# Operands of the first MoE's projection read straight into their low tiles, rounded on ScalarE, with the side weights and staged loads set wider apart in the attention

## The chip, the cores and the metric

The kernel runs on one core of one Trainium2 chip. The metric is the device time of one execution in microseconds (us). Of the kernel before there are three timed runs: 907.71, 910.16 and 914.64 us, median 910.16 us.

## The reference

Three layers in a row, all in float32: an attention with a decay bias, a mixture with a maximum of three products, and a mixture with a product of two.

```
scores = q @ k.T / sqrt(64);  bias = min(-(cum_i - cum_j), 0), cum = cumsum(max(s, 0))
attn = softmax(where(causal, scores + bias, -1e9)) @ v        # 4 batches, 8 heads, 576 x 64
x  = attn laid out as 2304 tokens x 512
h1 = max(x @ w1, x @ w2, x @ w3)                              # 2304 x 768
x2 = h1 @ w_out                                               # 2304 x 512, "the projection"
hT = (x2 @ w_a) * (x2 @ w_b)                                  # 2304 x 1536
out = hT @ w2_out                                             # 2304 x 512
```

## The kernel before

Every product of the MoE layers is made of three matmuls on TensorE: an operand `a` is split into `hi = round(a)` and `lo = a - hi` (the helper `hilo`: the rounding by `rnd` on ScalarE, letter A, or GpSimd, letter P; the subtraction always on VectorE), and `hi*hi + hi*lo + lo*hi` are added up in PSUM.

**Attention with the first MoE's gates (about 0 to 433 us).** Eight steps, one for a batch and one of its two ranges of rows (256 or 320 columns). A list called `stream` holds pairs of a position and a function: position 2.4 is 40% through step 2. It is sorted by position, and its functions are emitted in that order. The gates of a step (`gate`, 18 of them, 12 matmuls each, PSUM tile `g`, three banks) run one step later, as the other work of TensorE beside the attention of the next step; for each block of h1 ScalarE copies the first gate out of PSUM (L768), VectorE takes the maximum with the other two (L771), and ScalarE's queue sends the block to DRAM as `h1T` (L774). A scheduler then orders the instructions on each engine by priority and its own model of the time; each engine works its queue in that order. SyncE (SP) issues nearly all loads, in one queue.

Two kinds of side work stand in `stream` too. The **side weights** (w_out, six pieces, and two pieces of w_a and w_b) are loaded by `fetch_w1` into the ring `wst` of three buffers and turned to float32 by `load_side` (one instruction on ScalarE, two on VectorE); `w20_side` and `wsums` make sums and splits of them. The **staged sums**: the projection uses a scheme with seven products where eight would be needed (`OPS`, products 1, 2, 6, 5, 7, 4, 3), so four of its seven operands are sums of quarters of h1. For the first two of three blocks of 768 tokens, `stage_load` reads four quarters back from `h1T` into the one buffer `st`, `stage_sum` makes the four sums on VectorE and stores them as `h1S`; six such pieces (k = 0 to 5). Heads of the attention are loaded by `load_pair` (L510: `kraw`, the transposed keys), two pairs ahead, and split by `split_qk`, whose first instruction of the keys is a rounding on ScalarE into `KB`.

**The tail of the gates (400 to 433 us).** The last 18 gates run alone on TensorE. Beside them the seven operands of the projection's first block are read into the two buffers `hr` (`h_fetch`), rounded on ScalarE and GpSimd in turn (`HE`), and subtracted (`h0_make`); the weights of the projection are rounded on GpSimd (`wo1_make`).

**The projection (433 to 504 us).** `run_sb(sb)` makes a block of 768 tokens: seven products for each of two halves, 9 matmuls each (`chain`, L1115). The products 1, 6, 7, 4 add up in PSUM tile X, 2 in Y, 5 and 3 in Z, with one bank of each for either half, and a copy to `xt` by ScalarE (L1156, L1160, L1162, L1187) or an addition by VectorE between. Operands of the second block come through the four buffers `hrB` (`h1_fetch`), each rounded and subtracted into a slot A to F when the space for it is free (`freed`, `h_make`); those of the third through the same buffers, with four sums on VectorE (`h_sums`). `x0_split` splits the first block's result for the next layer.

**The second MoE (504 to 912 us)** follows the same pattern, and the change doesn't touch it.

Of the kernel before, what the change touches and what calls it, by code (L numbers as in the profile page):

```python
# [8 lines left out]
F32 = mybir.dt.float32  # L9
# [20 lines left out]
def kernel(  # L30
# [29 lines left out]
    P = 128  # L60
# [14 lines left out]
    def f(ap):  # L75
        return ap.bitcast(F32)
# [186 lines left out]
    side_keys = [("o", m) for m in range(MF)] + [("c", 0), ("c", 1)]  # L263
# [118 lines left out]
    def lpool(nm, **kw):  # L382
        return tc.alloc_tile_pool(name=nm, bufs=1, side="left", reuse_waits="tile", **kw)
# [35 lines left out]
    def wsums(p):  # L419
        def free(t, o):  # L420
            return t[:, o : o + KM * P].rearrange("r (k f) -> r k f", f=P)

        b11, b12, b21, b22 = (vblock(h, c, p) for h in range(2) for c in range(2))
        new = stg["w"].tile([P, 2, KM, P], F32, name=f"ws{p}")
        t5, t6, t4 = free(side_v[p], KM * WC), new[:, 0], new[:, 1]
        with tc.issue_after(done_sm[-1][0]), tc.issue_after(done_sm[-1][1]):
            tt("V", t5, b12, b11, ALU.subtract)
            tt("V", b12, b22, b12, ALU.subtract)
            tt("V", t6, b22, t5, ALU.subtract)
            tt("V", t4, b21, t6, ALU.subtract)  # L430
        wsrc[p] = {1: b11, 2: b21, 3: b22, 5: t5, 7: b12, 6: t6, 4: t4}

    wsrc = {}
# [11 lines left out]
    def w20_side(j):  # L445
        hi, lo = wm[0] if 0 in wm else w2_ops(rA, 0)
        v_ = [
            t[:, KM * WC :].rearrange("r (s c) -> r s c", s=2) for t in side_v
        ]
        with tc.issue_after(done_sm[-1][0]), tc.issue_after(done_sm[-1][1]):  # L450
            b_side(
                (v_[0][:, 0], v_[0][:, 1], v_[1][:, 0], v_[1][:, 1]),
                lambda i, q: hilo("P", hi[i], lo[i], q), (j,),
            )
# [484 lines left out]
    stream = []  # L939
# [55 lines left out]
    for j in range(ng):  # L995
        w_at = W0[j] if j < 3 else W0[3] + (W1 - W0[3]) * (j - 3) / (ng - 3)
        stream.append((w_at, 200, w_next))
    S1, S2 = 2.4, 3.4
    ns = len(side_keys)
    for j in range(ns):  # L1000
        stream.append((S1 + (S2 - S1) * j / ns, 200, w_next))
    for j in range(2):
        stream.append((S2 + 0.2 * (j + 1), 200, lambda j=j: w20_side(j)))
        stream.append((S2 + 0.2 * (j + 3), 200, lambda j=j: wsums(j)))
    stream.append((S2 + 0.5, 200, stage_open))
    for k in range(2 * KM):
        at = (4.4, 7.12)[k // KM] + 0.14 * (k % KM)
        stream.append((at, 200, lambda k=k: stage_load(k)))
        stream.append((at + 0.1, 200, lambda k=k: stage_sum(k)))
    stream.sort(key=lambda e: e[0])  # L1010
    for pos, off, fn in stream:
        if pos >= nsteps:
# [12 lines left out]
    ap_.release()  # L1025
    hs0 = {i: rpool(f"hs0_{i}") for i in reversed(OPS)}
    stg["x"].release()
    hr0 = lpool("hr0")

    hop = {}  # L1030

    HSRC = {1: 0, 2: 1, 4: 3, 6: 0, 5: 3, 7: 2, 3: 1}

    def h_read(dst, sb, i):
        if i in (1, 2, 4) or sb == 2:
            nc.sync.dma_start(dst, h_src(sb, HSRC[i]))
        else:
            nc.sync.dma_start(
                dst, h1S[sb, HSRC[i]].rearrange("p (k t) -> p k t", t=TB)
            )  # L1040
# [9 lines left out]
        h_tile(hs0[i], 0, i, i)  # L1050

    EN = "APAAPAP"
    HE = dict(zip(OPS, "APAPAPA"))
    hq = {}

    def h_fetch(i):
        hq[i] = hr0.tile([P, KM, TB], F32, tag="hr", bufs=2, name="hr")
        h_read(hq[i], 0, i)

    def h0_make(i):  # L1060
        hilo(HE[i], hop[0][0][i], hop[0][1][i], hq[i])

    moe = [m_next for _ in range(len(todo))]
    pieces = {0: lambda: (h_fetch(OPS[0]), h_fetch(OPS[1]))}
    for n, i in enumerate(OPS):
        def piece(n=n, i=i):
            h0_make(i)
            if n + 2 < len(OPS):
                h_fetch(OPS[n + 2])
        pieces[1 + n] = piece  # L1070
    for n, fn in enumerate(moe):
        with tc.high_priority(300):
            fn()
        if n in pieces:
            after(marks[-2], pieces[n])
    hr0.release()
    stg["w"].release()
    mp.release()
    for p_ in reversed(w1p):
# [7 lines left out]
    hrB = lpool("hrB")  # L1087
# [11 lines left out]

    def wo1_make(i):  # L1100
        for p in range(2):
            hilo("P", wo1[p][0][i], wo1[p][1][i], wsrc[p][i])

    with tc.high_priority(300):
        for n, i in enumerate(OPS):
# [21 lines left out]
    def behind(fn):  # L1127

        with tc.issue_after(last["A"]), tc.issue_after(last["V"]):
            fn()  # L1130
# [57 lines left out]
        )  # L1188

    def h_sums(part):  # L1190
        q = hq[2]
        if part:
            tt("V", q[:, 1], q[:, 1], q[:, 0], ALU.subtract)
            return
        tt("V", q[:, 3], q[:, 2], q[:, 3], ALU.add)
        tt("V", q[:, 2], q[:, 0], q[:, 2], ALU.subtract)
        tt("V", q[:, 0], q[:, 3], q[:, 0], ALU.subtract)

    def run_sb(sb, plan):
        us = [oproj(p, sb) for p in range(2)]  # L1200
        for n, i in enumerate(OPS):
            for u in us:
                u.prod(i)
            for fn in plan.get(i, ()):
                fn()
# [4 lines left out]
    }  # L1210
    slots1 = {}

    def h_make(sb, i):
        s_ = SLOT[sb][i]
        h_tile(slots1[s_], sb, i, s_)
        n = HSRC[i] if sb == 2 else hpos[i]
        hilo(HE[i], hop[sb][0][i], hop[sb][1][i], hq[2][:, n])

    def x0_split(part):
        q = [xt[:, 0, :, n] for n in range(4)]  # L1220
        behind(lambda: x2_split(0, 0, KH, q, EN, (part,)))

    for x in "ABC":
        slots1[x] = lpool(f"hs1{x}")
    hq[2] = hrB.tile([P, 4, KM, TB], F32, name="hrB")
    hpos = {i: n % 4 for n, i in enumerate(OPS)}

    def h1_fetch(i):
        h_read(hq[2][:, hpos[i]], 1, i)

    with tc.high_priority(300):
        for i in OPS[:4]:
            h1_fetch(i)
        for n in range(3):
            h_make(1, OPS[n])
            h1_fetch(OPS[n + 4])

    def freed(i, x=None, then=()):
        hs0[i].release()
        if x:  # L1240
            slots1[x] = lpool(f"hs1{x}")
        for j in then:
            h_make(1, j)

    run_sb(0, {
        1: [lambda: freed(1)],
        2: [lambda: freed(2, "D", (5,))],
        6: [lambda: freed(6, "E", (7,))],
        5: [lambda: freed(5, "F", (4,))],
        7: [lambda: freed(7)],  # L1250
        4: [lambda: freed(4)],
        3: [lambda: freed(3)],
    })
    vo.release()
    rA2 = rpool("rA2")
    xr = {0: rpool("xr0")}

    def h2_fetch(i):
        h_read(hq[2][:, HSRC[i]], 2, i)

    wpool = {0: rA}
    rawp = [rA2]
# [49 lines left out]
    def x2_split(sb, k0, k1, q, eng, part):  # L1312

        if sb not in xs:
            xs[sb] = {}, {}
            for i in (1, 2, 4, 6, 5, 7, 3):
                pool = xr1[{1: 0, 2: 0, 4: 1, 6: 2, 5: 2, 7: 3, 3: 3}[i]] if sb == 1 else xr[sb]
                for d, c in zip(xs[sb], "hl"):
                    d[i] = pool.tile([P, KH, TB], F32R, name=f"x{c}{sb}{i}")
        hi, lo = xs[sb]  # L1320
        es = dict(zip((1, 2, 4, 6, 5, 7, 3), eng))

        def sp(i, src):
            hilo(es[i], hi[i][:, k0:k1], lo[i][:, k0:k1], src)

        a_side(q, sp, part)

    coming.extend((wa[1], wb[1]))
    with tc.high_priority(100):
        more_raw(1)  # L1330
    run_sb(1, {
        1: [lambda: x0_split(0), lambda: h_make(1, 3), lambda: h2_fetch(1),
            lambda: h2_fetch(4), lambda: h_read(hq[2][:, 2], 2, 7), lambda: h2_fetch(2)],
        2: [lambda: h_make(2, 1)],
        6: [lambda: h_make(2, 4), lambda: h_sums(0)],
        5: [lambda: h_make(2, 2), lambda: h_sums(1)],
        7: [lambda: h_make(2, 6), lambda: x0_split(1)],
        4: [lambda: h_make(2, 5)],
        3: [lambda: h_make(2, 7)],
    })  # L1340
    run_sb(2, {1: [lambda: h_make(2, 3)]})
    strict[0] = False
    for x in "FEDCBA":
        slots1[x].release()
# [405 lines left out]
```

## Time and profile before

| | us |
|---|---|
| three timed runs | 907.71, 910.16, 914.64 |
| the profiled execution | 913.54 |
| its span, first to last instruction | 911.8 |
| TensorE busy | 887.0 |
| VectorE busy | 629.1 |
| ScalarE busy | 375.1 |
| GpSimd busy | 242.0 |

The profiled execution was 3.4 us longer than the median run. A matmul's busy time runs until its modelled end, so that matmuls in a dense row overlap; what counts on TensorE is where it has no matmul at all, and what clock it was granted (1.00 is 2.4 GHz, 0.50 is 1.2 GHz). In a row of the timeline the bracket says how long the engine was idle just before, and what released it; a release is inferred. "L341" is the subtraction, "L88" a rounding on GpSimd, "L81" one on ScalarE.

### The profile page before, as it was taken

The page shows a single profiled execution, that of the slowest core. Times are in us where ns is not written, and L with a number is a line of the kernel's source. Part 1 is how long each engine was busy: PE and PEld are TensorE (multiplying, and loading weights), DVE is VectorE, ACT ScalarE, POOL GpSimd, SP SyncE. Part 2 cuts the span into 40 slices and gives each one's busy share as a digit, 9 for nine tenths or more (in the row PEclk, how much of TensorE's full clock was granted, in tenths as well). Part 3 has the DMA queues.
Part 4 walks back from the last instruction along what each step waited for, and adds up shares of the span by engine and source line. Part 5 has one row for each costly group of instructions (what it writes and reads, how often), then busy time and mean ns, then how long its engine had stood idle before and what let it go on. Part 6 is the DMA issues. An engine that isn't in the chain of part 4 may idle for free.

```text
span 911.8 us, 16895 instructions
## 1 busy us (share of the span) xinstructions
PE 887.0 (97%) x6098; PEld 841.4 (92%) x6098; DVE 629.1 (69%) x1427; ACT 375.1 (41%) x829; POOL 242.0 (27%) x350
## 2 busy tenths in 40 slices
PE   7999999999999999999899999999999999999998
PEld 7677689999899999899799999999999999999998
DVE  4786466677656557535687967877776768996874
ACT  3654555555456555531333332322232323533321
POOL 6552233333123332214330302111111210321211
PEclk8999999999999999999999999999999999999999
DMA  6655273336631635336510114344443235254331
GB/s 186 209 206 183 77 217 92 116 100 202 194 94 56 182 100 186 115 90 218 162 51 26 53 61 153 137 165 147 155 146 129 99 111 185 69 169 160 102 116 47
DMA packets 68268, 120.04 MB, mean 132 GB/s; under 512 B 7017, under 2 KB 50697, under 8 KB 68185
## 3 DMA queue, kind: packets, MB, share of 16 engines
q1 hardware_dynamic: 61272, 111.88, 37.9%
q10 hardware_dynamic: 6912, 7.08, 2.4%
q8 instruction: 48, 0.79, 0.4%
q14 instruction: 36, 0.29, 0.1%
HBM read 87.90 MB, written 31.01 MB: 130 GB/s over the span
## 4 chain that ended last, share of the span: by engine, by line
PE 46%; DVE 3%; DMA 1%; POOL 1%; issue 1%; ACT 1%; POOLq 0%; ACTq 0%
PE X L1115 25%; PE Z L1115 13%; PE Y L1115 7%; DVE hl L341 1%; PE W L1115 1%; DMA hrB<-h1T 1%; DMA wraw<-in_moe_w_b_dram 1%; POOL hh L88 1%; DVE hrB L341 0%; DVE xl L341 0%; DVE xt L341 0%; ACT wraw L323 0%; POOL xh L88 0%; POOL wh L88 0%; DVE wval L328 0%
## 5 line engine op out<-in xcount | busy, mean ns | idle before, releaser
L762 PE MATMUL g<-Xh,hg 128*128 128x256 f32 (+1 forms) x576 | 174.3, 307 | 2.1 <-DVE hf L771 2.1
L762 PE MATMUL g<-Xl,hg 128*128 128x256 f32 (+1 forms) x576 | 174.0, 304 | 0.0
L762 PE MATMUL g<-Xh,lg 128*128 128x256 f32 (+1 forms) x576 | 172.8, 302 | 0.0
L762 PEld LDWEIGHTS g<-Xh,hg 128*128 128x128 f32 x576 | 108.6, 190 | 6.2 <-DVE hf L771 2.6
L762 PEld LDWEIGHTS g<-Xl,hg 128*128 128x128 f32 x576 | 109.5, 190 | 2.3 <-issue 0.9
L762 PEld LDWEIGHTS g<-Xh,lg 128*128 128x128 f32 x576 | 109.3, 190 | 2.0 <-issue 1.4
L1115 PE MATMUL X<-xh,wh 128*128 128x384 f32 x288 | 97.3, 338 | 0.1
L1115 PE MATMUL X<-xl,wh 128*128 128x384 f32 x288 | 96.9, 336 | 0.0
L1115 PE MATMUL X<-xh,wl 128*128 128x384 f32 x288 | 96.9, 337 | 0.0
L88 POOL TENSOR_SCALAR wh<-wval 128x256 fp32r<-128x256 f32 x77 | 40.5, 535 | 196.9 <-DVE wval L328 147.5
L580 POOL TENSOR_SCALAR P<-P,rs 128x128 f32<-128x128 f32 (+2 forms) x80 | 49.1, 619 | 108.3 <-DVE rs L575 82.8
L1115 PE MATMUL X<-woh,slot 128*128 128x256 f32 x408 | 76.6, 281 | 0.5 <-ACT ob L1162 0.5
L341 DVE TENSOR_TENSOR slot<-hraw,slot 128x768 fp32r<-128x768 f32 x60 | 60.4, 1033 | 13.8 <-POOL slot L88 11.0
L570 ACT ACTIVATE P<-P,nm 128x128 f32<-128x128 f32 (+2 forms) x80 | 46.6, 583 | 46.8 <-DVE nm L563 40.3
L341 DVE TENSOR_TENSOR u<-Z,u 128x384 f32<-128x384 f32 x72 | 39.6, 552 | 37.7 <-ACT u L1162 28.2
L1115 PEld LDWEIGHTS X<-woh,slot 128*128 128x128 f32 x408 | 64.3, 189 | 0.7 <-ACT ob L1162 0.7
L771 DVE TENSOR_TENSOR hf<-g,hf 128x256 f32<-128x256 f32 (+1 forms) x96 | 43.6, 454 | 28.8 <-PE g L762 18.6
L1115 PE MATMUL X<-wol,slot 128*128 128x256 f32 x204 | 56.9, 280 | 0.0
L1115 PEld LDWEIGHTS X<-xh,wh 128*128 128x128 f32 x288 | 54.1, 188 | 0.9 <-ACT s L1156 0.4
L1115 PEld LDWEIGHTS X<-xl,wh 128*128 128x128 f32 x288 | 54.1, 188 | 0.0
L1115 PEld LDWEIGHTS X<-xh,wl 128*128 128x128 f32 x288 | 54.0, 188 | 0.0
L81 ACT ACTIVATE slot<-hraw 128x768 fp32r<-128x768 f32 x39 | 32.5, 845 | 51.4 <-DVE hraw L341 24.4
(201 smaller groups left out, 2252.0 us busy)
## 6 DMA issues: line engine op xcount, KB each, us to landing
hT<-u SPq DMA_DIRECT2D x72, 192.0 KB
hraw<-hT SPq DMA_DIRECT2D x36, 384.0 KB
wraw<-in_moe_w_dram SPq DMA_DIRECT2D x18, 512.0 KB
wraw<-in_moe_w_out_dram SPq DMA_DIRECT2D x18, 512.0 KB
kraw<-in_kT_dram SPq DMA_DIRECT2D x24, 288.0 KB
wraw<-in_moe_w_a_dram SPq DMA_DIRECT2D x12, 512.0 KB
wraw<-in_moe_w_b_dram SPq DMA_DIRECT2D x12, 512.0 KB
st<-h1T SPq DMA_DIRECT2D x24, 192.0 KB
```

What stands on the lines that cost most here:

```text
L81: nc.scalar.activation(o, i, AF.Copy, scale=scale)
L88: nc.gpsimd.tensor_scalar(o, i, scale, 1.0, op0=ALU.mult, op1=ALU.mult)
L341: return {"V": nc.vector, "P": nc.gpsimd}[e].tensor_tensor(o, a, b, op=op)
L570: e_ = nc.scalar.activation(pt[:, c0:c1], pt[:, c0:c1], AF.Exp, bias=first, scale=-1.0, accum_out=sm[:, g : g + 1],)
L580: nc.gpsimd.tensor_scalar(pt[:, c0:c1], pt[:, c0:c1], rs[:, g : g + 1], 1.0, op0=ALU.mult, op1=ALU.mult,)
L762: nc.tensor.matmul(ps[:, :n], w[:, kk, :], x[:, kk, :], start=(i == 0), stop=(i == len(mm) - 1),)
L771: st["V"] = nc.vector.tensor_tensor(hf, ps[:, :n], hf, op=ALU.max)
L1115: e_ = nc.tensor.matmul(ps[:, :n], w, x, start=(first and i == 0), stop=(i == len(mm) - 1), skip_group_check=not first,)
```

## The change

Five edits. (1) Positions of the side work: the conversion of the side weights goes from 2.4 to 3.4 (eight pieces, 0.125 apart) to 2.8 to 4.9 (0.3 apart) with the loads fetched two pieces ahead by their own entries; their sums go from 3.6 to 4.2 to 5.2 to 5.8; the staged loads go from 4.4 and 7.12 on, 0.14 apart, to 5.95 on, 0.36 apart, and 7.12 on, 0.28 apart, and each sum comes 0.22 instead of 0.1 behind its load. (2) The first block's operands are read into the tile `lo` itself, all seven at once; ScalarE rounds `lo` into `hi`, and VectorE subtracts in place. The buffers `hr` are gone. (3) The second block's operands go the same way: three early, three (5, 7, 4) when their slot is free, with the roundings emitted together behind product 7, one (3) in the second block. (4) The buffers `hrB` hold only the third block's operands, read before the first block runs. (5) All roundings of the projection's operands, of its weights and of `x0_split` are ScalarE's.

```diff
-    S1, S2 = 2.4, 3.4
     for j in range(ns):
-        stream.append((S1 + (S2 - S1) * j / ns, 200, w_next))
+        stream.append((2.8 + 0.3 * j, 200, w_next))
+        if j + 2 < ns:
+            stream.append((2.81 + 0.3 * j, 200, lambda j=j: fetch_w1(side_keys[j + 2])))
     for j in range(2):
-        stream.append((S2 + 0.2 * (j + 1), 200, lambda j=j: w20_side(j)))
-        stream.append((S2 + 0.2 * (j + 3), 200, lambda j=j: wsums(j)))
-    stream.append((S2 + 0.5, 200, stage_open))
+        stream.append((2.4 + 0.2 * j, 200, lambda j=j: fetch_w1(side_keys[j])))
+        stream.append((5.2 + 0.2 * j, 200, lambda j=j: w20_side(j)))
+        stream.append((5.6 + 0.2 * j, 200, lambda j=j: wsums(j)))
+    stream.append((5.5, 200, stage_open))
     for k in range(2 * KM):
-        at = (4.4, 7.12)[k // KM] + 0.14 * (k % KM)
+        at = (5.95, 7.12)[k // KM] + (0.36, 0.28)[k // KM] * (k % KM)
         stream.append((at, 200, lambda k=k: stage_load(k)))
-        stream.append((at + 0.1, 200, lambda k=k: stage_sum(k)))
+        stream.append((at + 0.22, 200, lambda k=k: stage_sum(k)))
...
-    def h_fetch(i):
-        hq[i] = hr0.tile([P, KM, TB], F32, tag="hr", bufs=2, name="hr")
-        h_read(hq[i], 0, i)
-
-    def h0_make(i):
-        hilo(HE[i], hop[0][0][i], hop[0][1][i], hq[i])
+    def h_direct(sb, i):
+        hi, lo = hop[sb][0][i], hop[sb][1][i]
+        h_read(f(lo), sb, i)
+        return lambda: hilo("A", hi, lo, f(lo))
...
+    with tc.high_priority(300):
+        h0 = [h_direct(0, i) for i in OPS]
+    pieces = {2 + n: h0[n] for n in range(len(OPS))}
...
-            hilo("P", wo1[p][0][i], wo1[p][1][i], wsrc[p][i])
+            hilo("A", wo1[p][0][i], wo1[p][1][i], wsrc[p][i])
...
-        behind(lambda: x2_split(0, 0, KH, q, EN, (part,)))
+        behind(lambda: x2_split(0, 0, KH, q, "AAAAAAA", (part,)))
...
     with tc.high_priority(300):
-        for i in OPS[:4]:
-            h1_fetch(i)
-        for n in range(3):
-            h_make(1, OPS[n])
-            h1_fetch(OPS[n + 4])
+        for i in (1, 2, 6):
+            h1_make(i)
+        for i in (1, 4, 2, 7):
+            h_read(hq[:, HSRC[i]], 2, i)
...
         for j in then:
-            h_make(1, j)
+            h_slot(1, j)
+            h1_late.append(h_direct(1, j))
...
-        7: [lambda: freed(7)],
+        7: [lambda: freed(7), lambda: behind(lambda: [fn() for fn in h1_late])],
...
-        1: [lambda: x0_split(0), lambda: h_make(1, 3), lambda: h2_fetch(1),
-            lambda: h2_fetch(4), lambda: h_read(hq[2][:, 2], 2, 7), lambda: h2_fetch(2)],
+        1: [lambda: h1_make(3), lambda: x0_split(0)],
```

On SyncE's queue, at the first loads of transposed keys (about 117 us in the trace of before), the order moves so (minus: before, plus: the change):

```order
 L500 DMA kraw<-ck 1x2x256
 L501 DMA kraw<-ck 1x2x256
+L510 DMA kraw<-in_kT_dram 64x1152 x6
 L237 DMA wraw<-in_moe_w_out_dram 128x1024
-L510 DMA kraw<-in_kT_dram 64x1152 x2
+L506 DMA vraw<-in_qv_dram 128x640 x2
+L526 DMA QA_145<-qt 2x2x320
+L522 DMA KB_143<-kt 2x1152
 L237 DMA wraw<-in_moe_w_out_dram 128x1024
```

The six loads of keys, two for each pair of heads, now stand ahead of the side weight (`wraw`) that stood ahead of the first of them.

On ScalarE in the tail of the gates, before (`hh` is a rounded operand, `hf<-g` the copy of a first gate):

```order
L81 ACTIVATE hh_5339<-hr 128x1152
L768 COPY hf<-g 128x320 x2
L774 DMA h1T<-hf 128x320
L81 ACTIVATE hh_5343<-hr 128x1152
L768 COPY hf<-g 128x320
L774 DMA h1T<-hf 128x320
L768 COPY hf<-g 128x320
```

and in the change:

```order
L81 ACTIVATE hh_5336<-hl_5337 128x1152
L768 COPY hf<-g 128x320
L81 ACTIVATE hh_5338<-hl_5339 128x1152
L81 ACTIVATE hh_5340<-hl_5341 128x1152
L768 COPY hf<-g 128x320
L774 DMA h1T<-hf 128x320
L81 ACTIVATE hh_5342<-hl_5343 128x1152
L81 ACTIVATE hh_5344<-hl_5345 128x1152
L774 DMA h1T<-hf 128x320
L81 ACTIVATE hh_5346<-hl_5347 128x1152
L768 COPY hf<-g 128x320
```

One rounding stood ahead of the first two copies and a second one ahead of the third; now one stands ahead of the first, three ahead of the second and six ahead of the third.

On ScalarE in the projection's first block, before (the copies of products 1, 6, 7 and 4, L1156 to L1187, and the roundings between):

```order
L1156 COPY xt<-X 128x384 x2
L81 ACTIVATE hh_5853<-hrB 128x1152
L1160 COPY xt<-X 128x384 x2
L1162 COPY xt<-X 128x384 x2
L1187 COPY xt<-X 128x384 x2
```

and in the change (the same copies are L1148 to L1179):

```order
L1148 COPY xt<-X 128x384 x2
L81 ACTIVATE hh_5746<-hl_5747 128x1152
L1152 COPY xt<-X 128x384 x2
L81 ACTIVATE hh_5751<-hl_5752 128x1152
L1154 COPY xt<-X 128x384 x2
L81 ACTIVATE hh_5814<-hl_5815 128x1152
L81 ACTIVATE hh_5841<-hl_5842 128x1152
L81 ACTIVATE hh_5868<-hl_5869 128x1152
L1179 COPY xt<-X 128x384 x2
```

The roundings that fall into the first block's run now stand between all four pairs of copies; the three that wait for a freed slot come behind product 7's copies.

## Rows read from the trace of the kernel before

**Rows 1.** Page, busy time, share of the span and instructions of each engine.
```profile
PE 887.0 (97%) x6098; PEld 841.4 (92%) x6098; DVE 629.1 (69%) x1427; ACT 375.1 (41%) x829; POOL 242.0 (27%) x350
```

**Rows 2.** Stretches: length, busy PE, PEld, DVE, ACT, POOL, clock, DMA, GB/s.
```profile
126.00:129.00 3.00, 0.89 (x6) 0.63 (x6) 2.51 (x8) 2.70 (x9) 0.12 (x1) 1.00 0.19 47
130.00:134.00 4.00, 4.00 (x21) 3.97 (x20) 3.72 (x12) 1.84 (x5) 2.03 (x2) 0.57 0.90 272
240.00:242.00 2.00, 0.04 (x1) 0.02 (x1) 1.29 (x3) 0.00 (x0) 0.00 (x0) 1.00 0.14 54
243.00:247.00 4.00, 4.00 (x18) 4.00 (x18) 3.59 (x13) 3.47 (x9) 1.10 (x2) 0.60 0.75 255
372.00:376.00 4.00, 3.24 (x29) 3.07 (x28) 3.97 (x10) 3.07 (x7) 1.81 (x3) 1.00 0.57 200
444.00:448.00 4.00, 2.21 (x13) 1.95 (x12) 2.79 (x3) 1.98 (x4) 0.00 (x0) 1.00 0.88 238
452.00:456.00 4.00, 1.40 (x9) 1.11 (x8) 2.29 (x3) 1.70 (x3) 1.15 (x1) 1.00 0.11 25
476.00:480.00 4.00, 2.71 (x16) 2.39 (x15) 4.00 (x6) 1.03 (x3) 1.63 (x1) 1.00 0.00 0
488.00:492.00 4.00, 2.60 (x15) 2.28 (x14) 3.97 (x5) 0.86 (x2) 0.00 (x0) 1.00 0.00 0
```

**Rows 3.** Timeline, SyncE from 116 us and ScalarE at 125 us.
```profile
116.93 0.36 SPq L237 DMA_DIRECT2D wraw<-in_moe_w_out_dram  x1
117.40 1.20 SPq L510 DMA_DIRECT2D kraw<-in_kT_dram  x2
...
125.26 1.17 ACT L81 ACTIVATE KB<-kraw 128x1152 fp32r<-128x1152 f32 x1 [5.43 <-DMA kraw<-in_kT_dram]
```

**Rows 4.** Timeline, SyncE at 235 us, VectorE at 240 and 370 us.
```profile
235.15 2.03 SPq L402 DMA_DIRECT2D st<-h1T  x4
...
240.71 0.56 DVE L341 TENSOR_TENSOR st<-st 128x384 f32<-128x384 f32 x1 [3.88 <-DMA vraw<-in_qv_dram]
...
370.89 0.56 DVE L341 TENSOR_TENSOR st<-st 128x384 f32<-128x384 f32 x1 [3.19 <-DMA st<-h1T]
```

**Rows 5.** Who waited for whom, engine PE: us in total, times, longest.
```profile
PE Z L1115 <- DVE xt L341: 3.9, 2, 2.6
```

**Rows 6.** Timeline, 444 to 455 us: ScalarE, GpSimd, VectorE.
```profile
444.41 1.16 ACT L81 ACTIVATE hh<-hrB 128x1152 fp32r<-128x1152 f32 x1 [7.19 <-DMA hrB<-h1S]
445.48 0.84 ACT L1160 COPY xt<-X 128x384 f32<-128x384 f32 x2
...
452.01 1.15 POOL L88 TENSOR_SCALAR hh<-hrB 128x1152 fp32r<-128x1152 f32 x1 [12.19 <-DMA hrB<-h1T]
...
453.19 1.36 DVE L341 TENSOR_TENSOR hl<-hrB,hh 128x1152 fp32r<-128x1152 f32 x1 [6.23 <-POOL hh L88]
```

**Rows 7.** Timeline, 438 to 441 us: GpSimd and VectorE at the same time.
```profile
438.42 1.40 POOL L88 TENSOR_SCALAR hh<-hrB 128x1152 fp32r<-128x1152 f32 x1 [0.49 <-DVE wlo L341]
...
438.73 2.30 DVE L341 TENSOR_TENSOR hl<-hrB,hh 128x1152 fp32r<-128x1152 f32 x1
```

**Rows 8.** Timeline, 400 to 425 us: loads on SyncE, who took them, ScalarE's copies.
```profile
400.42 0.36 SPq L1036 DMA_DIRECT2D hr<-h1T  x1
404.41 1.15 POOL L88 TENSOR_SCALAR hh<-hr 128x1152 fp32r<-128x1152 f32 x1 [13.81 <-DMA hr<-h1T]
...
403.78 0.43 ACT L768 COPY hf<-g 128x320 f32<-128x320 f32 x1 [1.92 <-PE g L762]
...
411.99 0.43 ACT L768 COPY hf<-g 128x320 f32<-128x320 f32 x1 [3.01 <-PE g L762]
...
408.32 0.91 SPq L1036 DMA_DIRECT2D hrB<-h1T  x2
...
414.02 0.37 SPq L1036 DMA_DIRECT2D hr<-h1T  x1
...
424.31 1.64 POOL L88 TENSOR_SCALAR hh<-hr 128x1152 fp32r<-128x1152 f32 x1 [3.10 <-DMA hr<-h1T]
```

More of the change, by code (lines that the diff above doesn't have):

```diff
@@ L1027 @@
     stg["x"].release()
-    hr0 = lpool("hr0")
     hop = {}
@@ L1052 @@
     EN = "APAAPAP"
-    HE = dict(zip(OPS, "APAPAPA"))
-    hq = {}
-    def h_fetch(i):
-        hq[i] = hr0.tile([P, KM, TB], F32, tag="hr", bufs=2, name="hr")
-        h_read(hq[i], 0, i)
-    def h0_make(i):
-        hilo(HE[i], hop[0][0][i], hop[0][1][i], hq[i])
-    moe = [m_next for _ in range(len(todo))]
[L1064 to L1070, printed above, removed]
+    def h_direct(sb, i):
+        hi, lo = hop[sb][0][i], hop[sb][1][i]
+        h_read(f(lo), sb, i)
+        return lambda: hilo("A", hi, lo, f(lo))
+    moe = [m_next for _ in range(len(todo))]
+    with tc.high_priority(300):
+        h0 = [h_direct(0, i) for i in OPS]
+    pieces = {2 + n: h0[n] for n in range(len(OPS))}
     for n, fn in enumerate(moe):
@@ L1075 @@
             after(marks[-2], pieces[n])
-    hr0.release()
     stg["w"].release()
@@ L1190, in h_sums @@
     def h_sums(part):
-        q = hq[2]
+        q = hq
         if part:
@@ L1211, with h_slot, h1_make, h2_make @@
     slots1 = {}
-    def h_make(sb, i):
+    def h_slot(sb, i):
         s_ = SLOT[sb][i]
         h_tile(slots1[s_], sb, i, s_)
-        n = HSRC[i] if sb == 2 else hpos[i]
-        hilo(HE[i], hop[sb][0][i], hop[sb][1][i], hq[2][:, n])
+    def h1_make(i):
+        h_slot(1, i)
+        h_direct(1, i)()
+    def h2_make(i):
+        h_slot(2, i)
+        hilo("A", hop[2][0][i], hop[2][1][i], hq[:, HSRC[i]])
     def x0_split(part):
         q = [xt[:, 0, :, n] for n in range(4)]
-        behind(lambda: x2_split(0, 0, KH, q, EN, (part,)))
+        behind(lambda: x2_split(0, 0, KH, q, "AAAAAAA", (part,)))
     for x in "ABC":
         slots1[x] = lpool(f"hs1{x}")
[L1225 to L1229, printed above, removed]
+    hq = hrB.tile([P, 4, KM, TB], F32, name="hrB")
     with tc.high_priority(300):
-        for i in OPS[:4]:
-            h1_fetch(i)
-        for n in range(3):
-            h_make(1, OPS[n])
-            h1_fetch(OPS[n + 4])
+        for i in (1, 2, 6):
+            h1_make(i)
+        for i in (1, 4, 2, 7):
+            h_read(hq[:, HSRC[i]], 2, i)
+    h1_late = []
     def freed(i, x=None, then=()):
@@ L1331 @@
     run_sb(1, {
-        1: [lambda: x0_split(0), lambda: h_make(1, 3), lambda: h2_fetch(1),
-            lambda: h2_fetch(4), lambda: h_read(hq[2][:, 2], 2, 7), lambda: h2_fetch(2)],
[L1334 to L1339, printed above, removed]
+        1: [lambda: h1_make(3), lambda: x0_split(0)],
+        2: [lambda: h2_make(1)],
+        6: [lambda: h2_make(4), lambda: h_sums(0)],
+        5: [lambda: h2_make(2), lambda: h_sums(1)],
+        7: [lambda: h2_make(6), lambda: x0_split(1)],
+        4: [lambda: h2_make(5)],
+        3: [lambda: h2_make(7)],
     })
-    run_sb(2, {1: [lambda: h_make(2, 3)]})
+    run_sb(2, {1: [lambda: h2_make(3)]})
     strict[0] = False
```

2 lines of the change are left out of this document (removed).

## Prediction

> **What bounds the kernel now.** I read the page's busy times first: TensorE has matmuls for 887.0 of 911.8 us [rows 1], so no other engine is the bound as a whole, and the change, which leaves every matmul in place, can only win back stretches in which TensorE has none, or runs at the lower clock. There are 24.8 us without a matmul. The second view, the busy time by stretches, says where they lie in the part that the change touches; the reader is to compare the first two numbers of each row of [rows 2], the length and PE's busy time. In the attention: 126 to 129 us lacks 2.1 us, 240 to 242 us lacks 2.0, 372 to 376 us lacks 0.8. After the first two of these gaps the granted clock falls from its upper level, 2.4 GHz, to the lower, 1.2 GHz: 0.57 on average over 130 to 134 us, 0.60 over 243 to 247. In the projection four stretches lack 1.8, 2.6, 1.3 and 1.4 us; there the clock stays at 1.00. These make 12.0 us; the other half of the 24.8 us lies elsewhere, where the change moves nothing.
>
> The third view, the timeline of the engines that TensorE waits for, says why. At 126 us: ScalarE stood 5.43 us at the rounding of the keys into KB, until their load had landed at 125.26; that load had been issued at 117.40, right behind a side weight of 512 KB at 116.93 [rows 3]. The exponentials of the softmax are queued behind that rounding. At 240 and 371 us: VectorE stood 3.88 and 3.19 us at the first staged sum of a piece, whose loads had been issued from 235.15 on [rows 4], with the attention's subtraction Xl behind it. In the projection the list of waits has TensorE stop twice for VectorE's additions on Z, 3.9 us together [rows 5]; and the timeline has what held those and the copies: ScalarE waited 7.19 us for an operand's load before the two copies of product 6 could start at 445.48, GpSimd waited 12.19 us for another, and VectorE 6.23 us for GpSimd [rows 6]. So each of these gaps is one load that stands at the head of an in-order queue.
>
> **The change part by part.**
>
> Side weights. The keys' loads now stand ahead of the side weights on SyncE, and the conversions (one on ScalarE, two on VectorE, eight times, as many as before) are spread over two steps and fetched two pieces early. The gap at 126 us should go: 2.1 us, and 4.00 x (1 - 0.57) = 1.7 us of clock, together 3.8 us. The same 512 KB pieces now travel beside later loads of keys, one at a time.
>
> Staged loads. A sum comes 0.22 of a step behind its load where it came 0.1. The two waits of [rows 4] were 3.88 and 3.19 us with 0.1 of a step, some 5.6 us from issue to sum (235.15 to 240.71); twice the distance covers both. Gone: 2.0 us at 240 and 4.00 x (1 - 0.60) = 1.6 us of clock, 0.8 at 372, together 4.4 us. These pieces now lie in steps 5 to 7 instead of 4 and 7; the work is the same.
>
> Second block's operands. No `hrB` buffer has to come free first; the load that GpSimd waited for until 452.01 went into a buffer that two others had used. Three late loads still wait for space, but their roundings stand behind product 7's copies, where only product 4's copies are queued. Gone: the 1.8 and 2.6 us.
>
> Roundings on ScalarE. In the second block VectorE has the same list ahead of the two stops at 476 and 488 us, so it is late only if its own work takes too long. That it did: 2.30 us for a subtraction at 438.73 with GpSimd rounding from 438.42 on [rows 7], against 1.36 at 453.19, when GpSimd had just ended [rows 6]. GpSimd now has nothing here. The two stops, 1.3 and 1.4 us, should go; since VectorE's list stays as long, I leave half of them, 0.7 us (bounds 0 and 2.7).
>
> The Trainium skill (SBUF — State Buffer, Who interferes with whom) says that a VectorE instruction with two inputs in SBUF contends with a GpSimd instruction that reads SBUF, and that one of them waits for the whole of the other. By that rule the 0.94 us between the two rows would be a wait behind GpSimd's 1.40, and the whole of GpSimd's 1.6 us in 476 to 480 could come back to VectorE; the trace agrees as far as one pair of rows goes, and my 0.7 us would then be 0.
>
> The sum of what goes is 3.8 + 4.4 + 1.8 + 2.6 + 1.3 + 1.4 = 15.3 us.
>
> What is new. (a) In the tail of the gates all loads wait for the attention's space, so I take them as issued at 400.42, like the second `hr` load of before, which GpSimd had at 404.41: 4.0 us [rows 8]. Before, six loads from 408.32 on had landed by 424.31: after the first 4.0 us, 2.4 us each. So operand n lands at 404.4 + 2.4 (n - 1). With 1.16 us for a rounding [rows 6] the first copy out of PSUM starts at 405.6 instead of 403.78, 1.8 us late, and the third, behind six roundings, at 416.4 + 1.2 = 417.6 instead of 411.99, 5.6 us late. TensorE has two more PSUM banks to run into; from 403.78 to 411.99 it made six gates, 1.4 us each, so 2.7 us are covered. That makes 0 to 1.8 for the first copy and 0 to 2.9 for the third: bounds 0 and 4.7, and I take 1.5, since before, TensorE was also not stopped by copies that came late. Seven subtractions stand behind these roundings on VectorE with gates' maxima behind them; the same bank covers them. (b) Fourteen roundings of weights on ScalarE lie beside gates, and their cover is the same two banks. (c) New meetings of loads in the attention: bounds 0 and two gaps like that at 240 us, 2 x 3.6 = 7.2; I take 1.5, less than one half of one gap each, as the pieces are spread. A gain beyond 15.3 I exclude but for 1 us, as no other gap hangs on what is moved.
>
> So 15.3 - 0.7 - 1.5 - 1.5 = 11.6 us, from the profiled execution's 913.54: 901.9. The median run was 3.4 us shorter than that one. Of the gaps about half (12.0 of 24.8 us) are those that go, so I take half of the 3.4 us, 1.7, as already missing there, and the other half as lying elsewhere: 901.9 - 1.7 = 900.2 us.
>
> **The rivals.**
>
> VectorE and the loads of keys stay late: the work is only moved. VectorE's list in the second and third block is not shorter by one instruction, and the side weights still share the queue. For it: 4.00 of 4.00 us busy at 476 [rows 2]. Against it: GpSimd's share in that. Then 2.7 us stay in the projection and one gap of 3.6 us comes back in the attention: 900.2 + 2.0 + 3.6 - 1.5 = 904.3 us.
>
> The loads of the tail share the engines and land together. Then the first rounding starts when the seventh has landed, 404.4 + 6 x 2.4 = 418.8, the first copy at 420.0, 16.2 us late, of which 2.7 are covered: 13.5 us in place of the 1.5, and some 1.7 us of clock: 900.2 + 12.0 + 1.7 = 913.9 us. Against it: the load issued last, at 414.02, was among those that landed last [rows 8], as with a queue that is worked in order.
>
> The Trainium skill (DMA: Bandwidth & Descriptors, Queues, rings and completion order) says that each DMA engine takes descriptors in the order of the ring, but that completion is not first in, first out. By the first half the first operand would land first, by the second it need not; the trace agrees with the first half.
>
> Slower than before: the staged sums. Each piece's loads wait on SyncE for the store of the piece ahead, and each sum stands in VectorE's queue before the softmax. If every one of the six came before its loads, each would cost what the one at 240 us cost, 3.6 us: 21.6 us. Without the 4.4 us for these gaps the rest of the change gives 15.3 - 4.4 - 0.7 - 1.5 = 8.7 us, so it is slower from the third piece on, and with all six 910.16 + 21.6 - 8.7 = 923.1 us. For it: two of six waited before. Against it: twice the distance.
>
> **How the numbers follow.** The forecast has 0.62, from 895 (none of the 0.7, 1.5 and 1.5 us is paid, and the median's 3.4 us lie wholly elsewhere: 900.2 - 3.7 - 1.7 = 894.8) to 905 (5 us more of new waits). The first rival has 0.25, the second 0.06, the slower one 0.07, of which two parts in three lie over 1%. About 1% is what a measurement of this kernel tells from no change: 901.1 and 919.3 us. Below 901.1 lie some two thirds of the forecast's chance and a fifth of the first rival's: 0.46; above 919.3 some 0.05; the rest, 0.49, within 1%. The range reaches from 895 to 908.5, into the first rival and up to the second, and leaves out some 2 in 10. The chances of a gain hold most of it, so no second range is given.
>
> **What would show it.** Right: no row of under full busy time on PE at about 126, 240 and 372 us, and clock 1.00 after them; no wait of VectorE for GpSimd in the projection; PE's lacking time from 433 to 504 us at 1 us or so in place of 7.1. Wrong: ScalarE idle for a load of `hl` in the tail with TensorE idle behind it; VectorE idle at a staged sum; new stretches at the lower clock; or VectorE busy without a break up to a stop of TensorE on Z.

## The result, and the profile after

The changed kernel took 901.66 us (median of eight runs, 899.32 to 904.30) where the kernel before took 909.97 (eight runs on the same chip): ratio 0.9906, 95% interval 0.9883 to 0.9930, so 8.6 us less, between 6.4 and 10.6. The prediction was 900.2 with a range of 895 to 908.5. The profiled execution took 903.33 us, its span is 901.5.

The page's busy times, to be held against [rows 1]:

```profile
PE 886.2 (98%) x6098; PEld 840.1 (93%) x6098; DVE 624.9 (69%) x1427; ACT 392.8 (44%) x855; POOL 211.1 (23%) x324
```

TensorE has the same matmuls and is busy as long as before. 15.3 us of the span have no matmul, where it was 24.8. ScalarE has 18 us more and GpSimd 31 less: the roundings that moved. The busy time by stretches, with the columns of [rows 2]; the first six rows answer to rows there:

```profile
126.00:129.00 3.00, 3.00 (x23) 3.00 (x23) 2.63 (x11) 2.35 (x10) 0.83 (x2) 1.00 0.19 54
130.00:134.00 4.00, 4.00 (x31) 3.99 (x30) 1.14 (x3) 0.96 (x2) 0.50 (x1) 1.00 1.03 267
240.00:242.00 2.00, 2.00 (x15) 2.00 (x14) 1.33 (x5) 2.00 (x6) 1.38 (x3) 1.00 0.01 2
243.00:247.00 4.00, 4.00 (x32) 3.99 (x31) 2.31 (x5) 1.35 (x4) 0.59 (x1) 1.00 0.22 31
372.00:376.00 4.00, 4.00 (x35) 4.00 (x34) 3.59 (x12) 1.08 (x4) 1.42 (x2) 1.00 0.51 181
...
476.00:480.00 4.00, 4.00 (x24) 3.77 (x23) 4.00 (x5) 1.55 (x2) 0.00 (x0) 1.00 0.01 4
...
433.00:492.00 59.00, 58.84 (x337) 58.29 (x336) 42.49 (x49) 31.94 (x46) 1.95 (x3) 1.00 0.26 93
...
108.00:116.00 8.00, 8.00 (x37) 4.81 (x38) 2.34 (x13) 1.99 (x8) 1.69 (x5) 0.59 0.25 90
...
304.00:316.00 12.00, 10.80 (x78) 10.51 (x77) 7.19 (x27) 6.57 (x21) 3.60 (x8) 1.00 0.85 256
```

The reader is to see four things. At 126, 240 and 372 us TensorE's first two numbers are equal, and the clock behind them is 1.00. In the projection, 433 to 492 us now, 0.16 us lacks of what was 7.1, and that is the second MoE's first wait for a weight, which stood there before too. New is 0.59 of the clock over 108 to 116 us, about 3.3 us of time at a place that the change doesn't move (8.00 x (1 - 0.59)). New too is a stop of 1.20 us at 309. The timeline has its cause, together with a smaller stop at 328:

```profile
302.24 0.87 SPq L413 DMA_DIRECT2D h1S<-st  x2
...
306.40 1.75 SPq L402 DMA_DIRECT2D st<-h1T  x4
308.20 0.66 SPq L526 DMA_DIRECT2D QA<-kt  x1
...
310.79 0.38 PE L588 MATMUL s<-KB,QA 128*128 128x256 f32 x1 [1.20 <-DMA QA<-kt]
...
327.46 0.56 DVE L341 TENSOR_TENSOR st<-st 128x384 f32<-128x384 f32 x1 [4.05 <-DMA kraw<-in_kT_dram]
...
328.45 0.44 PE L587 MATMUL s<-KB,QA 128*128 128x384 f32 x1 [0.38 <-DVE nm L563]
```

The second staged load stands in SyncE's queue until the one buffer `st` is free of the piece ahead, from about 304 us to 306.40, and takes 1.75 us to issue; the small load of QA stands behind it and TensorE waits for it. And VectorE still stands 4.05 us at the third staged sum. The bracket names a load of keys, which came last by the profile; what the sum reads is the staged load, and a second profile of the same kernel names that one (4.06 us, `st<-h1T`). In the tail of the gates, ScalarE and SyncE's queue:

```profile
396.70 0.91 SPq L1037 DMA_DIRECT2D hl<-h1T  x2
397.71 1.67 SPq L1039 DMA_DIRECT2D hl<-h1S  x3
...
400.96 1.17 ACT L81 ACTIVATE hh<-hl 128x1152 fp32r<-128x1152 f32 x1 [3.94 <-DMA hl<-h1T]
402.03 0.41 ACT L768 COPY hf<-g 128x320 f32<-128x320 f32 x1
402.56 1.17 ACT L81 ACTIVATE hh<-hl 128x1152 fp32r<-128x1152 f32 x1
404.61 1.17 ACT L81 ACTIVATE hh<-hl 128x1152 fp32r<-128x1152 f32 x1 [0.88 <-DMA hl<-h1S]
...
402.49 0.42 PE L762 MATMUL g<-Xh,hg 128*128 128x320 f32 x1 [0.37 <-ACT hf L768]
```

The first copy of a gate stands behind a rounding that waits for its load, as predicted, but all of it is earlier and costs TensorE 0.37 us.

### The profile page after: what moved, and what is told of

Read it like the earlier page. It is cut to its first block, busy times and chain, and to the rows that moved or that the text cites. A ratio compares the mean times of both kernels' runs of the same rounds, so it can differ in the third digit from the quotient of the medians.

```text
span 901.5 us, 16886 instructions
## 1 busy us (share of the span) xinstructions
PE 886.2 (98%) x6098; PEld 840.1 (93%) x6098; DVE 624.9 (69%) x1427; ACT 392.8 (44%) x855; POOL 211.1 (23%) x324
## 4 chain that ended last, share of the span: by engine, by line
PE 89%; DMA 5%; DVE 2%; SPq 1%; issue 1%; ACT 1%; POOL 1%; ACTq 0%; DVEq 0%; POOLq 0%
PE X L1107 28%; PE g L762 22%; PE Z L1107 14%; PE Y L1107 7%; PE fpv L698 5%; PE t L714 3%; PE f L631 2%; PE s L587 2%; PE s L588 1%; PE W L1107 1%; PE ft L673 1%; PE tj L727 1%; PE sj L622 1%; PE sj L621 1%; DMA h1S<-st 1%
```

## The experiments

All kernels make the whole computation. Each is timed beside the kernel before on the same chip; ratios are to that. Theory A is the prediction's: each gap is one late load at the head of an in-order queue, and the edits are independent.

**The two halves of the change.** Edit 1 alone:

```diff
-        stream.append((S1 + (S2 - S1) * j / ns, 200, w_next))
+        stream.append((2.8 + 0.3 * j, 200, w_next))
...
-        at = (4.4, 7.12)[k // KM] + 0.14 * (k % KM)
+        at = (5.95, 7.12)[k // KM] + (0.36, 0.28)[k // KM] * (k % KM)
...
-        stream.append((at + 0.1, 200, lambda k=k: stage_sum(k)))
+        stream.append((at + 0.22, 200, lambda k=k: stage_sum(k)))
```

> The kernel before with edit 1 alone (positions of the side weights and staged loads). Theory A (each gap is one late load at the head of an in-order queue, and the edits are independent): the gaps at 126, 240 and 372 us go (4.8 us without a matmul and 3.3 us of clock), a wait of 1.2 us for QA at about 309 us comes, as in the changed kernel; the projection keeps its 7.1 us: 910.0 - 6.9 = 903.1 us. Theory B (the lower clock at 108 to 115 us in the changed kernel is the price of the new positions, about 3.3 us): 906.4 us, with that stretch at the lower clock here too.

And edits 2 to 5 alone, the same lines turned round in the changed kernel:

> The changed kernel with the positions of before, so edits 2 to 5 alone. Theory A: TensorE's 7.1 us without a matmul in the projection fall to 0.5 or less, the tail of the gates loses 0.4, and the gaps at 126, 240 and 372 us stand as before: 910.0 - 6.7 = 903.3 us. Theory B (the two halves need each other, since the staged loads meet the projection's): under 3 us of gain, above 907.

Measured: 907.55 us, ratio 0.9962 (0.9948 to 0.9976), 3.5 us less, for the positions; 907.00 us, 0.9956 (0.9939 to 0.9972), 4.0 us less, for the projection. Together 7.5 us, beside the change's 8.6: within the intervals (2.2 to 4.7, 2.6 to 5.6, 6.4 to 10.6 us) the halves add up, and nothing says that one needs the other. Both are some 3 us smaller than expected, and the time of the positions is the one that their theory B gave (3.6 us less). Its sign, the low clock at 108 us, is looked for in the stretches of the first:

```profile
108.00:116.00 8.00, 7.52 (x55) 5.75 (x54) 3.62 (x19) 4.22 (x15) 2.47 (x6) 1.00 0.49 161
126.00:136.00 10.00, 9.77 (x79) 8.19 (x78) 4.13 (x12) 4.55 (x12) 2.51 (x6) 1.00 0.77 217
...
304.00:316.00 12.00, 11.15 (x81) 10.85 (x81) 7.45 (x28) 5.79 (x19) 3.95 (x8) 1.00 0.87 259
324.00:334.00 10.00, 8.77 (x70) 7.33 (x69) 6.42 (x21) 4.11 (x10) 2.11 (x4) 1.00 0.69 207
...
433.00:504.00 71.00, 66.43 (x376) 64.89 (x375) 55.45 (x67) 24.84 (x40) 17.18 (x15) 1.00 0.25 85
```

and of the second:

```profile
108.00:116.00 8.00, 8.00 (x48) 5.36 (x48) 2.81 (x16) 3.82 (x13) 1.71 (x5) 0.80 0.47 151
126.00:136.00 10.00, 8.94 (x62) 8.43 (x61) 8.28 (x25) 7.38 (x21) 3.05 (x5) 1.00 0.89 250
...
433.00:492.00 59.00, 59.00 (x340) 59.00 (x339) 42.43 (x51) 31.91 (x48) 0.00 (x0) 1.00 0.26 91
```

The places are right: the new positions have no low clock at 108, and the projection's edits alone leave no stop from 433 to 492. The profiled execution of the positions was the fastest of their twelve; but over all twelve the granted clock is 0.995 in the mean, where the kernel before has 0.994 beside them, so the low clock isn't their price. The sizes are not right: with the old positions the gap at 126 to 136 us is 1.06 here and not 2.1, with no fall of the clock behind it, and with the old projection 4.57 us lack and not 7.1. Hence two more profiles of kernels already known.

**The same kernels once more.** Nothing edited.

> The kernel before once more, nothing edited, for a second profile of it. Theory A (the falls of the clock at 130 and 243 us belonged to that one execution, the gaps to the program): gaps within 0.7 us of 2.1 at 126 to 134, 2.0 at 240, 0.8 at 372 and 7.1 in the projection, with the clock at 1.00 behind at least one of the first two. Theory B (the falls belong to the program): clock of 0.6 over 130 to 134 and 243 to 247 us again.

> The changed kernel once more, nothing edited. Theory A (the lower clock at 108 to 115 us belongs to single executions): its gaps come at the same places within 0.5 us each (0.4 at about 403, 1.2 at 309, 0.4 at 328, under 0.3 in the projection), the clock after the gap at 105 us need not fall; 902.7 us beside a kernel before of 911.3. Theory B (it belongs to the change): the clock is at 0.5 over 108 to 115 us again.

The kernel before, stretches of the second profile:

```profile
108.00:116.00 8.00, 7.36 (x28) 4.02 (x29) 1.93 (x11) 2.34 (x9) 2.49 (x6) 0.54 0.37 116
126.00:136.00 10.00, 9.70 (x69) 9.39 (x69) 7.62 (x23) 6.26 (x16) 4.15 (x6) 1.00 0.77 207
230.00:248.00 18.00, 15.70 (x118) 13.81 (x116) 8.72 (x27) 5.48 (x13) 1.68 (x4) 1.00 0.70 204
...
433.00:504.00 71.00, 65.27 (x362) 63.73 (x360) 52.43 (x58) 25.57 (x40) 18.67 (x16) 0.98 0.25 80
```

The one run took 915.42 us. The gap at 126 us is 0.30 us here, with the clock at 1.00 behind it and behind the one at 240. The lower clock now lies over 108 to 116 us, in a kernel that has nothing of the change. So it belongs to neither program: theory A holds for the clock, and was wrong that the gap at 126 is steady and that 7.1 us lack in the projection, which are 5.7 here. The changed kernel again took 901.68 us (0.9889, 0.9868 to 0.9911), with its stops at the same places within 0.5 us (0.73 at 309) and the low clock over 108 to 116 once more (0.59). Taken by itself that is what theory B expected; against it stand the kernel before, which had it too, and four kernels with the new places (the positions alone and the next two runs among them) whose profiles have 1.00 there.

**GpSimd's share.** The change with its roundings in turns again:

```diff
-        return lambda: hilo("A", hi, lo, f(lo))
+        return lambda: hilo(HE[i], hi, lo, f(lo))
...
-            hilo("A", wo1[p][0][i], wo1[p][1][i], wsrc[p][i])
+            hilo("P", wo1[p][0][i], wo1[p][1][i], wsrc[p][i])
...
-        behind(lambda: x2_split(0, 0, KH, q, "AAAAAAA", (part,)))
+        behind(lambda: x2_split(0, 0, KH, q, EN, (part,)))
```

> The changed kernel with the roundings of the projection's operands, of its weights and of x0_split in turns with GpSimd again, as before the change; loads and slots stay those of the change. Theory A (VectorE was slowed by GpSimd): subtractions of 1.36 us come to 1.9 to 2.3 beside GpSimd's roundings, and the stops at about 476 and 488 us in the old count come back, 2.7 us: 904.4 us. Theory B (the direct loads alone made the gain): 901.7 us within 1, with no stop of TensorE over 0.5 us in the projection.

Measured: 905.73 us, 0.9943 (0.9927 to 0.9959). VectorE, GpSimd and TensorE in the second block, from the timeline:

```profile
459.18 1.34 DVE L341 TENSOR_TENSOR hl<-hl,hh 128x1152 fp32r<-128x1152 f32 x1
...
461.32 4.20 DVE L341 TENSOR_TENSOR hl<-hrB,hh 128x1152 fp32r<-128x1152 f32 x2
465.56 2.19 DVE L341 TENSOR_TENSOR hrB<-hrB 128x1152 f32<-128x1152 f32 x1
...
460.46 1.96 POOL L88 TENSOR_SCALAR hh<-hrB 128x1152 fp32r<-128x1152 f32 x1 [3.34 <-ACT xt L1153]
462.38 1.93 POOL L88 TENSOR_SCALAR xh<-xt 128x768 fp32r<-128x768 f32 x1
464.28 2.26 POOL L88 TENSOR_SCALAR hh<-hrB 128x1152 fp32r<-128x1152 f32 x1
...
470.81 0.44 PE L1108 MATMUL Z<-hh,who 128*128 128x384 f32 x1 [1.14 <-DVE xt L341]
482.04 0.44 PE L1108 MATMUL X<-hl,who 128*128 128x384 f32 x1 [1.40 <-DVE hl L341]
```

Two subtractions beside GpSimd take 2.10 us each, a third operation 2.19, where one alone takes 1.34: some 2.4 us more. VectorE has no break from there to the second stop, and TensorE's two stops, 1.14 and 1.40, are back; the other two of the projection are not. Theory A. GpSimd is slowed too: a rounding of that size took 1.16 us elsewhere in this run, 2.26 here. That the two contend agrees with the rule of the Trainium skill (SBUF — State Buffer, Who interferes with whom) that the prediction weighed. That one of them waits for the whole of the other, as the prediction put it, these rows don't show: 1.16 us on top of 1.34 would be 2.50, and both engines take longer.

**Distance or place of the staged sums.** The change with the sums as near behind their loads as before:

```diff
-        stream.append((at + 0.22, 200, lambda k=k: stage_sum(k)))
+        stream.append((at + 0.1, 200, lambda k=k: stage_sum(k)))
```

> The changed kernel with each staged sum 0.1 of a step behind its load, as before the change, instead of 0.22; the positions of the loads stay. Theory A (the distance is what removed the waits): VectorE waits 3 to 4 us at two or more of the six sums and TensorE stops behind it: 901.7 + 4.4 = 906 us or more. Theory B (the new places of the loads removed them, where the queue of loads is emptier): no wait over 1 us, 901.7 us within 1.

Measured: 904.61 us, 0.9931 (0.9913 to 0.9949), 2 to 4 us over the change. One sum in six waits, the third:

```profile
328.59 2.34 DVE L341 TENSOR_TENSOR st<-st 128x384 f32<-128x384 f32 x4 [5.47 <-DMA st<-h1T]
...
331.36 0.44 PE L587 MATMUL s<-KB,QA 128*128 128x384 f32 x1 [2.36 <-DVE nm L563]
```

Neither theory in full: the distance is worth 2.0 us at this one sum (2.36 against 0.38), and the other five have no wait at the old distance either. Two of them, the second and the sixth, had one of 3.1 to 4.0 us in the old places, so for these the new place did it.

**Staged sums alone, side weights alone.** The kernel before with only the last two pairs of lines of edit 1's diff above:

> The kernel before with the staged loads and sums alone at their new places and distance; the side weights stay at 2.4 to 3.4. Theory A (staged sums and side weights each cause their own gap): the gaps at 240 and 372 us go (2.0 and 1.2 us), one wait for QA at about 309 us (0.9) and one sum late at about 327 us (1.2) come, the gap at 126 to 134 us stays: within 1.5 us of the kernel before, and of the 3.5 us of all new positions 2 or more are the side weights'. Theory B (the staged sums' new distance is what pays): 3 us or more faster than before.

and the change with the side weights' loads, conversions and sums put back:

```diff
-        stream.append((2.8 + 0.3 * j, 200, w_next))
+        stream.append((S1 + (S2 - S1) * j / ns, 200, w_next))
...
-        stream.append((5.2 + 0.2 * j, 200, lambda j=j: w20_side(j)))
+        stream.append((S2 + 0.2 * (j + 1), 200, lambda j=j: w20_side(j)))
```

> The changed kernel with the side weights' loads, conversions and sums at the positions of before; staged sums and projection stay those of the change. Theory A (the side weights' new positions are worth what the gap at 126 to 134 us costs, 1.5 us on average over four profiles with the old positions, and about 0.9 of clock): slower than the change by 1 to 3 us, 903.5 to 905.5 beside a kernel before of 912. Theory B (they give nothing, as positions together gained no more than the staged ones alone): 901.7 within 1, with a gap at 126 to 134 us and none at 309 or 328.

Measured: 907.44 us, 0.9950 (0.9932 to 0.9968), 4.6 us less, for the staged sums alone, as much as for all positions: theory B. And 902.59 us, 0.9909 (0.9886 to 0.9932), without the side weights' part, not to be told from the change. As it stands that time is theory B's, with the gap that it named; but the kernel before took 910.3 us beside it, where the expectation reckoned with 912, and against the change's second ratio (0.9889) it is 1.8 us more, which is theory A's. The noise of that difference is some 3 us, so what the side weights' new places give by themselves is not decided; the 3.8 us of the prediction aren't seen. TensorE and ScalarE at the keys, from the timeline of the staged sums alone:

```profile
131.68 0.42 PE L762 MATMUL g<-Xh,hg 128*128 128x320 f32 x1 [2.44 <-DVE hf L771]
...
128.27 1.17 ACT L81 ACTIVATE KB<-kraw 128x1152 fp32r<-128x1152 f32 x1 [5.77 <-DMA kraw<-in_kT_dram]
```

and of the change with the old side weights:

```profile
129.57 0.41 PE L762 MATMUL g<-Xh,hg 128*128 128x320 f32 x1 [0.62 <-DVE hf L771]
...
126.15 1.17 ACT L81 ACTIVATE KB<-kraw 128x1152 fp32r<-128x1152 f32 x1 [3.94 <-DMA kraw<-in_kT_dram]
```

The order of VectorE's, TensorE's and SyncE's instructions is the same in both up to the tail of the gates, so the difference is one of executions. ScalarE's wait of 3.94 us costs TensorE 0.62 there (and 0.61 four us later), that of 5.77 costs 2.44. The last section has what differs: the clock at 108 us.

**A better order.** The stops at 309 and 328 us are the staged loads' own. Edit to the change:

```diff
-        stream.append((at, 200, lambda k=k: stage_load(k)))
-        stream.append((at + 0.22, 200, lambda k=k: stage_sum(k)))
+        stream.append(((5.95, 6.31, 6.67, 7.12, 7.4, 7.68)[k], 50, lambda k=k: stage_load(k)))
+        stream.append(((6.17, 6.53, 7.05, 7.34, 7.62, 7.9)[k], 200, lambda k=k: stage_sum(k)))
```

> The changed kernel with two more edits: the staged loads have priority 50 instead of 200, so that on the queue of loads the two of QA and KB at about 308 us stand ahead of the staged load that waits for the one buffer; and the third sum comes 0.38 of a step behind its load instead of 0.22. Theory A (the wait for QA at 309 us and VectorE's 4 us at 327 us are the price of the staged sums' places): both go, 1.6 us, 901.1 us where the change has 902.7. Theory B (the wait moves to the next staged piece or to the tail): within 0.5 us of the change.

the same with the old side weights:

> The run with the staged loads behind QA and KB and the later third sum, with the side weights at the positions of before as well. Theory A: slower by 1 to 3 us than that run with the new positions (900.7): 901.7 to 903.7. Theory B: 900.7 within 1.

and, on top of the first, a later rounding in the tail:

```diff
-    pieces = {2 + n: h0[n] for n in range(len(OPS))}
+    pieces = {3 + n: h0[n] for n in range(len(OPS))}
```

> The run with the staged loads behind QA and KB and the later third sum, and one edit more: in the tail of the gates the roundings come one gate later (3 + n instead of 2 + n), so that ScalarE's first copy of a gate stands ahead of the first rounding. Theory A (TensorE's stop at about 401 us is that copy waiting behind a rounding that waits for its load): the stop of 0.1 to 1.1 us goes: 900.0 within 1. Theory B (the roundings come too late for the projection instead): a new stop at the projection's first products, 1 us or more.

Measured: 900.72 us, 0.9872 (0.9849 to 0.9896); 901.14 us, 0.9887 (0.9867 to 0.9907); 898.80 us, 0.9859 (0.9835 to 0.9883). In the first the stop at 309 is 0.36 us and the one at 328 gone, theory A (its slowest run, 900.90 us, is below the fastest of the change on that chip, 901.32), but the tail's stop is 1.12:

```profile
400.93 0.42 PE L762 MATMUL g<-Xh,hg 128*128 128x320 f32 x1 [1.12 <-ACT hf L768]
```

The last has the copy ahead of the rounding:

```profile
398.26 0.43 ACT L768 COPY hf<-g 128x320 f32<-128x320 f32 x1 [3.85 <-PE g L762]
398.58 2.26 ACT L81 ACTIVATE hh<-hl 128x1152 fp32r<-128x1152 f32 x2
...
398.74 0.41 PE L762 MATMUL g<-Xh,hg 128*128 128x320 f32 x1 [0.22 <-ACT hf L768]
```

and no new stop in the projection (58.84 of 59.00 us busy, as in the change): theory A, though the time is 0.2 us below what it allowed. This last order took 12.8 us less than the kernel before (10.7 to 15.0). Against the change it was not timed on one chip: its slowest run took 899.52 us where the fastest of the change's fourteen took 899.32, but its granted clock was 0.996 in the mean and the change's 0.994, which is up to 2 of the 2.9 us between the medians. The second, with the old side weights, is again not to be told from the one with the new: 0.4 us more as it stands (theory B), 1.4 by the ratios (near theory A).

## Why the prediction was right, and by which terms

**The mechanism held.** The forecast's case came true, not the rivals': nothing was only moved (0.16 us lacks in the projection), the tail's loads did not land together (the first rounding began at 400.96 us, the third at 404.61), and one staged sum waited, not three or six. Of the four signs of being wrong that it named, though, three were seen, each at a small price: ScalarE idle 3.94 us for a load of `hl` (0.37 us on TensorE), VectorE idle 4.05 us at a staged sum (0.38 us), and a new stretch at the lower clock, which the kernel before can have too. Several terms were off, and that the sum still came within 2 us is in part luck, since their errors partly cancelled.

**The path at 126 us: right in the load, wrong behind it.** TensorE did not stop there for the exponentials. It waited for a maximum of VectorE's, which stood behind VectorE's own part of splitting the keys, and that behind ScalarE's rounding; in the trace of before:

```profile
126.46 1.36 DVE L92 TENSOR_TENSOR KB<-kraw,KB 64x1152 fp32r<-64x1152 f32 x1 [4.82 <-ACT KB L81]
...
128.67 0.41 PE L762 MATMUL g<-Xh,hg 128*128 128x320 f32 x1 [2.11 <-DVE hf L771]
```

**Side weights, "2.1 us, and 4.00 x (1 - 0.57) = 1.7 us of clock, together 3.8 us": too large.** Six profiles have the old side weights; at 126 to 136 us they lack 2.11, 0.30, 1.06, 2.44, 1.23 and 0.96 us, 1.35 in the mean, and the clock fell behind two of them. With the new places it is 0.44 or less in seven profiles, 0.15 in the mean. That is 1.2 us and some 0.6 of clock: 1.8. Against it, over 304 to 316 and 324 to 334 us together, the four profiles with the new side weights and the change's staged sums lack 1.1 to 2.1 us, the two with the old side weights 0.16 and 0.34. So, as far as these profiles show, what is won at 126 is lost again at 309 and 328; the times leave it open. Why the side weights make the staged loads' places worse was not tried.

**Staged loads, 4.4 us: right in sum**, 4.6 alone (2.9 to 6.2), but by other terms. The stretches at 230 to 248 and 368 to 377 us lacked 2.7 to 3.5 us together in the three profiles with the old places, 3.2 in the mean where 2.8 was counted, and nothing in the ten with the new. The fall of the clock at 243 us, counted as 1.6, stands in one of the three, 0.5 in the mean: 3.7 in all. And the prediction's "two of six waited before" overlooked a third: VectorE stood 3.11 us at 230.54 too, where TensorE lost nothing in that execution, but 0.62 and 0.35 us in two others. The reason given, "twice the distance covers both", was only part of it: five sums have no wait at the old distance in the new places, and the third has one of 3.2 to 4.9 us at the new.

**The projection, 1.8 + 2.6 + 1.3 + 1.4 = 7.1 us: right in kind, too large.** Over 433 to 504 us the four profiles with the old projection lack 7.24, 5.73, 5.62 and 4.57 us, 5.8 in the mean; the one first read was the worst. The part that is GpSimd's is steady, 2.5 to 2.7 us wherever its roundings are there. The 0.7 us left for VectorE should have been 0.

**The tail, 1.5 us: bounds right, the working wrong.** The loads were issued from 396.70 us on, not at 400.42. The first was there 4.3 us later, where 4.0 was taken, and the third rounding began at 404.61: less than 2 us from load to load, where 2.4 was taken. The stop, one copy late behind one rounding, was 0 to 1.26 us in the seven profiles that have this tail, 0.7 in the mean.

**New meetings in the attention, 1.5 us: right**, 1.2 and 0.4, as a load behind another on SyncE and as a late sum, and 1.7 in the mean of the four profiles.

**From the profiled execution to the median, "I take half of the 3.4 us": open.** The two falls of the clock, 3.3 us, stood at these places in that execution, but other executions have falls elsewhere: its granted clock, 0.993, is 0.001 below the mean of 41 other runs of the kernel before, some 0.9 us. Where the rest of the 3.4 us lies is not known.

Put together, 4.0 us too much gain (2.0 at the side weights, 0.7 at the staged loads, 1.3 in the projection) stand against 1.5 us too much cost (0.7 at VectorE, 0.8 in the tail) and 0.2 too little (the new meetings). So 11.6 becomes 8.9 us, where the change measured 8.6 and, the second time, 10.1. Of the 8.9 us 1.1 are clock (0.6 and 0.5), and even these aren't seen in the mean: over 41 runs of the kernel before and 14 of the change the granted clock is 0.994 in both. Without them the sum is 7.8 us; the first measurement's interval (6.4 to 10.6) holds both, the second's (8.1 to 12.0) 8.9 alone.

## What to carry to other kernels

A gap that hangs on one load at the head of an in-order queue is cured by the load's place, but another load then stands there: look at what is queued right behind the moved one, here a load of 4 KB behind a staged one that waited for its buffer. Read the size of a gap from two profiles or more before it goes into a sum, and look at what the clock did ahead of it; leave a fall of the clock out of what an edit gives back unless every profile has it. Where GpSimd's roundings lengthen VectorE's subtractions (2.10 us in place of 1.34) and VectorE is near the critical path, rounding on a third engine that is idle can be worth more than sharing the work.

## What was not expected of the hardware

The clock's falls are a matter of the single execution. In all thirteen profiles TensorE lacks 1.8 to 2.2 us between 103 and 111 us, where no edit has yet moved an instruction; in seven of them the clock then goes to its lower level, 1.2 GHz, and in six it stays at 1.00. It fell behind 1.82 us and stayed behind 2.03. In the projection of the kernel before it fell behind a gap of 1.82 us in the second profile and stayed behind 2.6 at the same place in the first. Of the seven falls at 108 us four took 1.6 to 1.7 us of TensorE's work (8.00 x (1 - 0.79) with the clock of 108 to 116 us), the two of the change 3.3, and that in the second profile of before 5 (17.00 x (1 - 0.70), over 103 to 120 us).

Here such a fall was partly paid back at the next gap that hung on a load. Six profiles have the old side weights, and in them the order of the instructions is the same on every engine up to 145 us:

| profile | clock, 108 to 116 us | lacking on TensorE, 126 to 136 us | ScalarE's wait for the keys |
|---|---|---|---|
| the staged sums alone | 1.00 | 2.44 | 5.77 |
| the kernel before, first | 1.00 | 2.11 | 5.43 |
| the change with the old side weights | 0.79 | 1.23 | 3.94 |
| the projection's edits alone | 0.80 | 1.06 | 3.77 |
| the better order with the old side weights | 0.79 | 0.96 | 3.66 |
| the kernel before, second | 0.54 | 0.30 | 2.73 |

Counted from the end of the stop at about 108 us, the keys were there after 17.4 to 18.4 us in the first five. TensorE came to its stop after 19.0 and 19.3 us where the clock had stayed, and after 20.5 us where it had fallen: later by most of what the fall took, so that less was left to wait for. The gap at 126 us and the fall at 108 are thus no two independent terms, and a gap that differs from one profile to the next need not be the load's doing.
